# A gated mix of linear attention and a token MLP: the order and the queues of the first loads

## The chip, the cores and the metric

The kernel runs on one core of a Trainium2 chip. The metric is the device time of one execution in microseconds (us), as the median of several runs. A core has TensorE (PE in the profile: matmuls; PEld: its weight loads), VectorE (DVE), ScalarE (ACT), GpSimd (POOL) and SyncE (SP, which here only issues copies). Copies between the chip's memory and the core's buffers are carried out by 16 DMA engines; SP and ScalarE each have a queue of their own on which they issue them.

## The reference

For x of 2048 tokens by 512 features (bfloat16) the output is `g * a + (1 - g) * b`:

- `g = sigmoid(sum(x * gate_w))`, one number for each token.
- `a` is linear attention with 32 heads of 16 features: q, k, v from `x @ wqkv`, the feature map `phi(t) = where(t > 0, t + 1, exp(t)) + 1e-6` on q and k, `num = phi(q) @ (phi(k)^T v)`, divided by `phi(q) . sum(phi(k))`, then `@ wo`.
- `b` is an MLP over the tokens: `h = layernorm(x)` over the features, `u = gelu(h^T @ w1 + b1)` with w1 of 2048 by 1792, `y = u @ w2 + b2`, turned back.

So the first layer of the MLP sums over all 2048 tokens, and it needs the layernorm of every token before it ends.

## The kernel before

The 2048 tokens are 16 tiles of 128 (t = 0 to 15). A tile of x is 128 by 512 (128 KB); a tile of w1 in the first half of its columns, `w1A`, is 128 by 896 (224 KB).

The kernel begins with the MLP's first layer, first half. Seven accumulators `accA` (banks of TensorE's accumulation memory) each collect one 128-column block of w1A over the tokens. The loop over the first 12 tiles (lines 271 to 273) does seven matmuls for each tile, one to an accumulator; the last 4 tiles are done accumulator by accumulator, and each accumulator goes through a Gelu on ScalarE when it is complete. Then come the k projection with the sum `phi(k)^T x`, the second half of the first layer with the q projection between its blocks, and the second layer with the attention's output added in the same accumulators.

The matmuls of tile t need `xh[t]`, the normalised tile, and `w1A[t]`. The layernorm runs on VectorE, with one step on ScalarE: statistics (`bn_stats`, line 196), their aggregation (line 199), the standard deviation (Sqrt on ScalarE, line 201), its reciprocal (line 207) and the normalisation (line 209, written as "apply" here). VectorE's order is written out (lines 217 to 231): the statistics of tile t come before the apply of tile t - 1; for tiles 1 to 3 the statistics are in two halves, one before and one behind that apply. Instructions run in that order on each engine, so an apply waits for the next tile of x too.

Ahead of the matmuls stand 18 warm-up matmuls on a constant (line 183) and `vps` (line 186), a small matmul with an identity that turns 30 rows of bias (`b_rows`: 14 rows of b1, 16 rows of b2) into columns. Two copies on ScalarE (lines 229 and 230) move the result into `b1_sb` and `b2_sb` after the standard deviation of tile 1.

The copies in, all issued through `load` (line 124), are in program order on each queue. On ScalarE's queue: the rows of b1, the first 128 columns of w1A tile 0, the rows of b2; behind them on ScalarE come the load of the table for Sqrt and a first use of it. On the sync queue: x 0, x 1, the rest of w1A 0, and then x t + 1 and w1A t in turn; then the gate's row, the k weights, 16 transposing copies of x and the rest of the weights. The framework gives copies one of eight completion semaphores in turn, in the order of the program over both queues, and a copy waits on its queue until the copy eight before it has landed.

Of the kernel before, what the change touches and what calls it, by code (L numbers as in the profile page):

```python
# [16 lines left out]
def kernel(  # L17
# [13 lines left out]
    nc = tc.nc  # L31
    P = nc.NUM_PARTITIONS
# [9 lines left out]
    NT = S // P  # L42
    ND = D // P
    NF = F // P
# [4 lines left out]
    FA = NFA * P  # L49
    TAIL = 4  # L50

    x_view = X.rearrange("(t p) d -> p t d", p=P)
    o_view = O.rearrange("(t p) d -> p t d", p=P)
    wqkv_view = A_wqkv.rearrange("(k p) n -> p k n", p=P)
    w1_view = B_w1.rearrange("(t p) f -> p t f", p=P)
    w2_view = B_w2.rearrange("(f p) s -> p f s", p=P)
    b1_view = B_b1.rearrange("(f p) -> f p", p=P)
    b2_view = B_b2.rearrange("(t p) -> t p", p=P)
# [8 lines left out]
    def ptile(shape, dt, name):  # L67
        return persist.tile(shape, dt, name=name, tag=name)

    def bank(name):  # L70
        return psum.tile([P, SC], FP32, name=name, tag="bank")

    def mm(o, lhsT, rhs, start, stop, **kw):
        tc.keep_in_program_order(
            nc.tensor.matmul(o, lhsT=lhsT, rhs=rhs, start=start, stop=stop, **kw)  # L75
        )

    xr = ptile([P, NT, D], BF16, "xr")
# [17 lines left out]
    ident = ptile([P, P], BF16, "ident")  # L96
    gw_b = ptile([P, D], BF16, "gw_b")
    b_rows = ptile([NF + NT, P], BF16, "b_rows")
    b1_sb = ptile([P, NF], FP32, "b1_sb")
    b2_sb = ptile([P, NT], FP32, "b2_sb")  # L100
# [17 lines left out]
    w1A = wpool.tile([P, NT, FA], BF16, name="w1A", tag="w")  # L118
    w1B = wpool.tile([P, NT, FA], BF16, name="w1B", tag="w")

    pin = tc.keep_in_program_order

    def load(o, i, eng=None, **kw):
        pin((eng or nc.sync).dma_start(out=o, in_=i, **kw))

    def load_x(t0, t1):
        load(xr[:, t0:t1, :], x_view[:, t0:t1, :])

    def load_w1a(t):
        load(w1A[:, t, :], w1_view[:, t, 0:FA])  # L130


    tbl = work.tile([P, 1], FP32, name="tbl", tag="tbl", bufs=2)
    load(b_rows[0:NF, :], b1_view, nc.scalar)
    load(w1A[:, 0, 0:P], w1_view[:, 0, 0:P], nc.scalar)
    load(b_rows[NF : NF + NT, :], b2_view, nc.scalar)
    pin(nc.scalar.activation(out=tbl[:], in_=eps_t[:], func=ACT.Sqrt))

    load_x(0, 1)
    load_x(1, 2)  # L140
    load(w1A[:, 0, P:FA], w1_view[:, 0, P:FA])
    for t in range(1, NT):
        if t + 1 < NT:
            load_x(t + 1, t + 2)
        load_w1a(t)
    load(gw_b[:], gw_row_view.to_broadcast([P, D]))
    load(wk_sb[:], wqkv_view[:, :, D : 2 * D])
    for c in range(NSC):
# [11 lines left out]
    for j in range(ND):  # L160
# [10 lines left out]
        out=mask[:], in_=mask[:], compare_op=ALU.is_gt, fill=1.0,  # L171
# [3 lines left out]
        out=mask[:], in_=mask[:], compare_op=ALU.is_ge, fill=0.0,  # L175
# [4 lines left out]

    warm_ps = bank("warm_ps")
    one = nc.const_aps.tensor(1.0, [P, 256], BF16)
    for _ in range(18):
        mm(warm_ps[:, :256], one[:, 0:P], one, True, True)
    vps = bank("vps")
    mm(vps[:, : NF + NT], b_rows[:], ident[0 : NF + NT, 0 : NF + NT], True, True)

    BS = nc.vector.BN_STATS_DIM  # L190
# [2 lines left out]
    def ln_bn(t, d0, d1, h, parts):  # L193
        if h == 0:
            stats[t] = work.tile([P, parts, BS], FP32, name="stats", tag=f"stats{parts}", bufs=4)
        pin(nc.vector.bn_stats(out=stats[t][:, h, :], in_=xr[:, t, d0:d1]))  # L196

    def ln_aggr(t):
        pin(nc.vector.bn_aggr(out=mv[:, t, :], in_=stats[t][:]))
        pin(  # L200
            nc.scalar.activation(
                out=sd[:, t : t + 1], in_=mv[:, t, 1:2], func=ACT.Sqrt, bias=eps_t[:], scale=1.0
            )
        )

    def ln_apply(t):
        pin(nc.vector.reciprocal(out=rstd[:, t : t + 1], in_=sd[:, t : t + 1]))
        pin(
            nc.vector.tensor_scalar(
                out=xh[:, t, :], in0=xr[:, t, :],  # L210
                scalar1=mv[:, t, 0:1], scalar2=rstd[:, t : t + 1],
                op0=ALU.subtract, op1=ALU.mult,
            )
        )
# [4 lines left out]
    for t in range(1, NT):  # L219
        if t < HALVES:  # L220
            ln_bn(t, 0, D // 2, 0, 2)
            ln_apply(t - 1)
            ln_bn(t, D // 2, D, 1, 2)
        else:
            ln_bn(t, 0, D, 0, 1)
            ln_apply(t - 1)
        ln_aggr(t)
        if t == 1:
            pin(nc.scalar.copy(out=b1_sb[:], in_=vps[:, :NF]))
            pin(nc.scalar.copy(out=b2_sb[:], in_=vps[:, NF : NF + NT]))  # L230
    ln_apply(NT - 1)


    tbl = work.tile([P, 1], FP32, name="tbl", tag="tbl", bufs=2)
# [22 lines left out]
    def gelu(acc, j):  # L257
        pin(
            nc.scalar.activation(
                out=uT[:, j, :], in_=acc[:], func=ACT.Gelu_apprx_tanh,  # L260
                bias=b1_sb[:, j : j + 1], scale=1.0,
            )
        )
# [4 lines left out]
    def mlp1(acc, w, col, t, last):  # L268
        mm(acc[:], w[:, t, col : col + P], xh[:, t, :], t == 0, last)

    for t in range(NT - TAIL):
        for j in range(NFA):
            mlp1(accA[j], w1A, j * P, t, False)
    for j in range(NFA):
        for t in range(NT - TAIL, NT):
            mlp1(accA[j], w1A, j * P, t, t == NT - 1)
        gelu(accA[j], j)
# [53 lines left out]
    for i in range(ND):  # L331
# [4 lines left out]
            out=z_parts[:, 1, :], in0=zacc[:], in1=z_parts[:, 0, :], op=ALU.subtract  # L336
# [214 lines left out]
    t = NT - 1  # L551
# [35 lines left out]
```

## Time and profile before

| | us |
|---|---|
| median of 3 runs (163.14 to 163.45) | 163.24 |
| the profiled execution | 163.19 |
| its span, first to last instruction | 161.5 |
| TensorE busy with matmuls | 156.9 (97%) |
| VectorE busy | 117.6 (73%) |
| ScalarE busy | 53.1 (33%) |

The profile is of one execution. Busy time is counted by instruction; matmuls are pipelined and their ends are modelled, so their rate is read from the distance of their starts. The chain of work that ended last goes back from the last instruction, at each step to what released it. A line of the timeline has the start and the duration in us, the engine, the line of the kernel, the operation, what it writes and reads, the shape and the count, and in brackets the idle time before it and what ended it. An engine's name with a q (SPq, ACTq) is its issuing part: such a line is the issue of a copy, not its transfer.

### The profile page before, as it was taken

How to read it: one execution, taken by the hardware profiler on the slowest of the kernel's cores; microseconds unless marked ns; L12 is line 12 of the kernel's file. 1: busy time of each engine (PE TensorE's matmuls, PEld its weight loads, DVE VectorE, ACT ScalarE, POOL GpSimd, SP SyncE). 2: the span in 40 equal slices, each digit the busy share in tenths (PEclk: the TensorE clock that was granted, in tenths of full speed). 3: DMA queues.
4: the chain of work that ended last, by engine and by line, in shares of the span. 5: the costliest groups of instructions: out<-in, count | busy, mean ns of one | idle time of the engine just before them, and what ended most of it. 6: DMA issues, size and time to landing. Idle time of an engine off the chain costs nothing.

```text
span 161.5 us, 2192 instructions
## 1 busy us (share of the span) xinstructions
PE 156.9 (97%) x775; PEld 73.0 (45%) x789; DVE 117.6 (73%) x272; ACT 53.1 (33%) x91; POOL 1.5 (1%) x10
## 2 busy tenths in 40 slices
PE   7999999999999999999999999999999999999992
PEld 5444444444444445444444444444444444444452
DVE  2999989999999997998959999999999900000002
ACT  3222258962332124261348730000008330150140
POOL 3000000000000000000000000000000000000000
PEclk9999999999999999999999999999999999999999
DMA  4999996445699942169930103999445367360021
GB/s 139 279 351 341 335 186 139 108 105 102 165 394 380 265 136 81 37 211 381 334 67 0 39 32 80 345 392 296 153 69 162 91 196 233 71 189 4 0 97 33
DMA packets 36806, 28.33 MB, mean 175 GB/s; under 512 B 20412, under 2 KB 33084, under 8 KB 36796
## 3 DMA queue, kind: packets, MB, share of 16 engines
q1 hardware_dynamic: 36320, 27.90, 58.7%
q10 hardware_dynamic: 476, 0.30, 0.6%
q8 instruction: 6, 0.10, 0.3%
q14 instruction: 4, 0.03, 0.1%
HBM read 19.28 MB, written 4.46 MB: 147 GB/s over the span
## 4 chain that ended last, share of the span: by engine, by line
PE 97%; issue 1%; DVE 0%; DVEq 0%
PE yps L75 38%; PE accA L75 15%; PE accB L75 15%; PE qacc L75 9%; PE kacc L75 9%; PE Gps L75 8%; PE warm_ps L75 2%; PE kvps L75 0%; DVE ot L531 0%; PE w2ps L75 0%; PE vps L75 0%; DVEq L531 0%
## 5 line engine op out<-in xcount | busy, mean ns | idle before, releaser
L75 PE MATMUL yps<-uT,w2h 128*128 128x512 bf16 (+2 forms) x234 | 49.0, 366 | 0.2
L75 PEld LDWEIGHTS <-w2h 128*128 128x128 bf16 x238 | 22.8, 98 | 25.9
L524 ACT ACTIVATE ot<-yps,c,c 128x512 bf16<-128x512 f32 x15 | 11.5, 777 | 46.9 <-DVE pq L400 24.4
L75 PE MATMUL accB<-xh,w1B 128*128 128x512 bf16 x110 | 24.9, 379 | 0.1
L75 PE MATMUL accA<-xh,w1A 128*128 128x512 bf16 x110 | 24.4, 381 | 0.1
L531 DVE TENSOR_SCALAR ot<-yps,c,c 128x384 bf16<-128x384 f32 (+1 forms) x2 | 1.1, 544 | 29.0 <-PE yps L75 29.0
L75 PEld LDWEIGHTS <-xT 128*128 128x128 bf16 x128 | 12.4, 98 | 14.9 <-issue 0.2
L75 PEld LDWEIGHTS <-w1B 128*128 128x128 bf16 x112 | 10.9, 98 | 13.2
L75 PEld LDWEIGHTS <-w1A 128*128 128x128 bf16 x112 | 10.9, 98 | 13.2 <-issue 0.4
L75 PE MATMUL kacc<-wk_sb,xT 128*128 128x512 bf16 x63 | 15.7, 379 | 0.1
L75 PE MATMUL Gps<-pk,xr 128*128 128x512 bf16 x62 | 15.5, 379 | 0.1
L75 PE MATMUL yps<-W2sb,pqT 128*128 128x512 bf16 (+2 forms) x67 | 14.6, 366 | 0.1
L75 PE MATMUL qacc<-wq_sb,xT 128*128 128x512 bf16 x62 | 14.4, 379 | 0.1
L282 ACT ACTIVATE e<-qacc 128x512 bf16<-128x512 f32 x16 | 9.6, 597 | 12.2 <-PE qacc L75 8.0
L282 ACT ACTIVATE e<-kacc 128x512 bf16<-128x512 f32 x16 | 9.2, 598 | 12.7 <-PE kacc L75 7.0
L196 DVE BATCH_NORM_STATS2 stats<-xr 128x6 f32<-128x512 bf16 (+1 forms) x19 | 11.1, 582 | 2.1 <-DMA xr<-in_A_x_dram 2.1
L400 DVE SCALAR_TENSOR_TENSOR pq<-pq,odds,rd 128x512 bf16<-128x512 bf16 x16 | 12.0, 752 | 0.6
L396 DVE TENSOR_REDUCE den<-prod 128x32 f32<-128x544 f32 x16 | 11.5, 720 | 0.6
L289 DVE SCALAR_TENSOR_TENSOR pk<-kacc,e 128x512 bf16<-128x512 f32 x16 | 11.1, 692 | 1.0
L289 DVE SCALAR_TENSOR_TENSOR pq<-qacc,e 128x512 bf16<-128x512 f32 x16 | 11.1, 692 | 0.6
L241 DVE CUSTOM_DVE_ANT_0 junk<-xr,gw_b 128x512 bf16<-128x512 bf16 x16 | 11.0, 690 | 0.5
L284 DVE TENSOR_SCALAR e<-e 128x512 bf16<-128x512 bf16 x32 | 9.2, 288 | 2.8 <-ACT e L282 2.4
(54 smaller groups left out, 95.3 us busy)
## 6 DMA issues: line engine op xcount, KB each, us to landing
w2h<-in_B_w_dram SPq DMA_DIRECT2D x4, 1792.0 KB, 7.7
w1B<-in_B_w_dram SPq DMA_DIRECT2D x4, 896.0 KB, 8.3
w1A<-in_B_w_dram SPq DMA_DIRECT2D x15, 224.0 KB, 4.2
xr<-in_A_x_dram SPq DMA_DIRECT2D x16, 128.0 KB, 3.9
q_dram<-pq SPq DMA_DIRECT2D x16, 128.0 KB, 1.8
out_dram<-ot SPq DMA_DIRECT2D x15, 128.0 KB, 1.8
wk_sb<-in_A_wqkv_dram SPq DMA_DIRECT2D x1, 512.0 KB, 7.0
wv_sb<-in_A_wqkv_dram SPq DMA_DIRECT2D x1, 512.0 KB, 13.5
```

Of the source, the lines that this page charges most:

```text
L75: nc.tensor.matmul(o, lhsT=lhsT, rhs=rhs, start=start, stop=stop, **kw)
L196: pin(nc.vector.bn_stats(out=stats[t][:, h, :], in_=xr[:, t, d0:d1]))
L241: nc.vector.tensor_tensor_reduce(out=junk[:], in0=xr[:, t, :], in1=gw_b[:], scale=1.0, scalar=0.0, op0=ALU.mult, op1=ALU.add, accum_out=gp ...
L282: pin(nc.scalar.activation(out=e[:], in_=acc[:], func=ACT.Exp))
L284: nc.vector.tensor_scalar(out=e[:], in0=e[:], scalar1=1.0, scalar2=PHI_EPS, op0=ALU.min, op1=ALU.add)
L289: nc.vector.scalar_tensor_tensor(out=o, in0=acc[:], scalar=0.0, in1=e[:], op0=ALU.max, op1=ALU.add)
L396: pin(nc.vector.tensor_reduce(out=den[:], in_=prod[:], op=ALU.add, axis=AX.X))
L400: nc.vector.scalar_tensor_tensor(out=heads, in0=heads, scalar=odds[:, t : t + 1], in1=rd[:].unsqueeze(2).to_broadcast([P, NH, HEAD]), op0= ...
L524: nc.scalar.activation(out=ot[:, d0:d1], in_=yps[:, d0:d1], func=ACT.Identity, scale=c1[:, t : t + 1], bias=c2[:, t : t + 1],)
L531: nc.vector.tensor_scalar(out=ot[:, d0:d1], in0=yps[:, d0:d1], scalar1=c1[:, t : t + 1], scalar2=c2[:, t : t + 1], op0=ALU.mult, op1=ALU.add,)
```

## The change

x tile 0 is loaded as two halves of 64 tokens, the first on the sync queue, the second on ScalarE's; x tile 1 comes whole on ScalarE's queue, behind that half. The sync queue then carries w1A 0 (now one copy) and w1A 1, and from t = 2 on x t and w1A t in turn. The two copies of bias rows go on the sync queue behind w1A 3. One warm-up matmul is dropped. The matmul `vps` moves behind the seven matmuls of tile 8, and the two copies to `b1_sb` and `b2_sb` come, on ScalarE, behind the load of the Gelu table and before the first Gelu.

```diff
-    load(b_rows[0:NF, :], b1_view, nc.scalar)
-    load(w1A[:, 0, 0:P], w1_view[:, 0, 0:P], nc.scalar)
-    load(b_rows[NF : NF + NT, :], b2_view, nc.scalar)
+    HP = P // 2
+    load(xr[0:HP, 0, :], x_view[0:HP, 0, :])
+    load(xr[HP:P, 0, :], x_view[HP:P, 0, :], nc.scalar)
+    load(xr[:, 1, :], x_view[:, 1, :], nc.scalar)
     pin(nc.scalar.activation(out=tbl[:], in_=eps_t[:], func=ACT.Sqrt))
-
-    load_x(0, 1)
-    load_x(1, 2)
-    load(w1A[:, 0, P:FA], w1_view[:, 0, P:FA])
-    for t in range(1, NT):
-        if t + 1 < NT:
-            load_x(t + 1, t + 2)
+    load_w1a(0)
+    load_w1a(1)
+    for t in range(2, NT):
+        load_x(t, t + 1)
         load_w1a(t)
+        if t == 3:
+            load(b_rows[0:NF, :], b1_view)
+            load(b_rows[NF : NF + NT, :], b2_view)
...
-    for _ in range(18):
+    for _ in range(17):
         mm(warm_ps[:, :256], one[:, 0:P], one, True, True)
-    vps = bank("vps")
-    mm(vps[:, : NF + NT], b_rows[:], ident[0 : NF + NT, 0 : NF + NT], True, True)
...
         ln_aggr(t)
-        if t == 1:
-            pin(nc.scalar.copy(out=b1_sb[:], in_=vps[:, :NF]))
-            pin(nc.scalar.copy(out=b2_sb[:], in_=vps[:, NF : NF + NT]))
     ln_apply(NT - 1)
...
     for t in range(NT - TAIL):
         for j in range(NFA):
             mlp1(accA[j], w1A, j * P, t, False)
+        if t == NT // 2:
+
+            vps = bank("vps")
+            mm(vps[:, : NF + NT], b_rows[:], ident[0 : NF + NT, 0 : NF + NT], True, True)
+            pin(nc.scalar.copy(out=b1_sb[:], in_=vps[:, :NF]))
+            pin(nc.scalar.copy(out=b2_sb[:], in_=vps[:, NF : NF + NT]))
```

## The prediction

> **What bounds the kernel now.** I read the page's busy line first, then the chain that ended last, then the timeline of the first 24 us, then the landing times of the single copies there.
>
> ```profile
> PE 156.9 (97%) x775; PEld 73.0 (45%) x789; DVE 117.6 (73%) x272; ACT 53.1 (33%) x91; POOL 1.5 (1%) x10
> ...
> 0.83 4.00 PE warm_ps L75 x18
> 4.86 0.18 PE vps L75
> 5.03 6.77 PE accA L75 x30
> ```
>
> TensorE (PE) is busy 97% of the span and the chain runs through it from 0.83 us on. Nothing in the change takes a matmul of the computation away, so it can act only on the moment at which the first layer (accA) runs without a gap. What sets that moment stands in the timeline (start, duration, engine):
>
> ```profile
> 0.79 0.67 ACTq L124 DMA_DIRECT2D b_rows<-in_B_b_dram  x1
> 1.49 0.37 ACTq L124 DMA_DIRECT2D w1A<-in_B_w_dram  x1
> 2.19 0.43 SPq L124 DMA_DIRECT2D xr<-in_A_x_dram  x1
> 3.01 0.69 DVE L196 BATCH_NORM_STATS2 stats<-xr 128x6 f32<-128x512 bf16 x1 [2.08 <-DMA xr<-in_A_x_dram]
> 3.84 0.40 DVE L196 BATCH_NORM_STATS2 stats<-xr 128x6 f32<-128x256 bf16 x1
> 4.28 0.16 DVE L207 RECIPROCAL rstd<-sd 128x1 f32<-128x1 f32 x1
> 4.34 0.33 SPq L124 DMA_DIRECT2D xr<-in_A_x_dram  x1
> 4.48 0.41 DVE L209 TENSOR_SCALAR xh<-xr,mv,rstd 128x512 bf16<-128x512 bf16 x1
> 4.96 11.37 PE L75 MATMUL accA<-xh,w1A 128*128 128x512 bf16 x50
> 5.39 0.37 DVE L196 BATCH_NORM_STATS2 stats<-xr 128x6 f32<-128x256 bf16 x1
> 6.97 0.43 DVE L196 BATCH_NORM_STATS2 stats<-xr 128x6 f32<-128x256 bf16 x1
> 8.50 0.64 DVE L196 BATCH_NORM_STATS2 stats<-xr 128x6 f32<-128x512 bf16 x1
> 9.24 0.41 DVE L209 TENSOR_SCALAR xh<-xr,mv,rstd 128x512 bf16<-128x512 bf16 x1
> 9.70 6.35 PEld L75 LDWEIGHTS <-w1A 128*128 128x128 bf16 x30 [0.15 <-issue]
> ```
>
> VectorE (DVE) idles 2.08 us for x tile 0, then works without a pause to the end of xh tile 3 at 9.24 + 0.41 = 9.65. The first statistics on x tiles 1, 2, 3 and 4 stand at 3.84, 5.39, 6.97 and 8.50; each x tile has landed by then. PE starts tile 0 at 4.96, just after xh 0 (4.89), and tile 3 at 9.70, just after xh 3 (9.65), where its weight load shows the only pause. A tile costs PE seven matmuls of 0.216 us (24.38 us for 112), 1.51 us, and DVE, once whole-tile statistics begin, 1.18 us (12.77 minus 11.59, two starts of the apply). So from tile 4 on DVE gains on PE. **The path is x tile 0 to tile 3 through DVE; whatever delays DVE there delays the end one for one.** It returns once: xh 15 is ready at 23.27 + 0.41 = 23.68 and PE wants it at 9.70 + 66 x 0.216 = 23.95, a cover of 0.27 us.
>
> The landings, as KB and us from issue to landing:
>
> ```profile
> w1A<-in_B_w_dram ACTq DMA_DIRECT2D x1, 32.0 KB, 2.8
> ...
> b_rows<-in_B_b_dram ACTq DMA_DIRECT2D x1, 4.0 KB, 2.8
> ```
>
> Single copies on the sync queue (SP), from the trace's answers on xr and w1A over narrow stretches: x 0 2.2, x 1 2.2 (lands 3.5), x 2 2.9 (5.1), w1 1 3.9 (6.6), w1 2 4.0 (7.6), x 4 3.7 (8.0), w1 3 3.9 (8.6). The DMA engines are already 0.80, 0.93, 0.78, 0.90, 0.97 busy in the five microseconds from 2 to 7.
>
> **The change, part by part.**
>
> *x tile 0 in halves.* The halves' statistics wait for both. Each half's issue can take SP's 0.40 to 0.43; ScalarE's first copy took 0.67. If that 0.67 belongs to the queue's first copy, the second half is no earlier than now (landing 2.99); if not, half the rows behind each issue save at most about half of the 0.40 us that one issue takes, 0.2 us. Gain 0 to 0.2; I take 0.1, between. It is worth something only if x 1 is there too, because the DVE order puts statistics of x 1 ahead of the apply of tile 0.
>
> *x tile 1 on ScalarE's queue.* It is issued second there: at 1.49 (after 0.67) or about 1.25 (after 0.43), instead of 1.26 on SP. Landing after 2.2 us (SP's first copies) gives 3.5 to 3.7; after 2.8 us (both measured copies of this queue) 4.1 to 4.3. The nearest rows are this queue's, and those were smaller copies: I take 4.1. DVE then starts at 4.12 instead of 3.84: +0.28 for xh 0 (5.17).
>
> *w1 tiles 0 and 1 ahead of x 2.* x 2 is still the fourth copy on SP, at 2.19, but now has x 0, x 1, all of w1 0 and w1 1 before it: 224 KB more. In the trace of before that same set of copies ends with w1 1 at 6.6, when part of x 3 had been moved too; its bytes (some 850 kB) were moved by about 5.4 (262 + 275 + 203 kB in the stretches from 2 to 5, then 271 per us), and x 2 itself landed about 0.7 us behind its bytes, which gives 6.1. Two queues issue the set 0.47 us (one SP slot) sooner, which, used fully, gives 5.6. At best nothing is lost (5.1). I take 5.8, between 5.6 and 6.1, against a need of 5.39: **+0.4 us on DVE**, which takes in the 0.28 of x 1. Likewise x 3 now takes the place of w1 2 (7.6, less 0.47: 7.1) against 6.97, and x 4 that of w1 3 plus the bias rows: +0.2 and about +0.4, the same shift, not added to it.
>
> *Bias rows behind tile 3.* Two issues on SP, 0.43 each (ScalarE's rows: 0.67 and 0.44), ahead of x 4, w1 4 and all later copies. x 4 is the tenth copy instead of the eighth: 0.79 + 9 x 0.47 = 5.02, up to 5.26, instead of 4.34; with 3.7 us it lands at 8.7 to 9.0. Needed at 8.50 + 0.4 = 8.9, so covered by the shift already counted, or a 0.1 more. x 5 goes from 5.18 to about 6.0, landing 9.7, needed at 9.66 + 0.4: covered. Each ninth copy waits for the landing of the one eight before it (the SP waits on w1A landings are 2.0 us in all, seven times), so later ones follow the landings, not the count. The gate row, wk and the transposes move by at most a slot, 0.5 us; the eighth transpose is issued near 28.4, lands 2.8 later and is wanted at 32.8, 1.6 us of cover.
>
> *vps moves from before tile 0 to behind tile 8.* Before, it ran 4.86 to 4.96 while PE waited for xh 0 anyway: removing it gains nothing unless xh 0 comes before 4.9. Behind tile 8 PE has no gap, so its place is paid: 0.11 us (from its start to the next matmul) at most, and at least 0.02 (a 64-column matmul of kvps, 32 in 0.62 us). The 128-column weight load after it needs about 0.1 (98 ns) and a 30-column matmul can't hide it: **+0.1 us**. The bias rows have landed long before (18.5 us against about 9).
>
> *The two bias copies on ScalarE* (0.15 and 0.17) now stand after the Gelu table load and ahead of the seven Gelus. The first Gelu starts 0.3 later; a Gelu takes 0.72, its accumulator comes each 0.86, so the lag is gone after three. No PE instruction waits for it. Cost 0.
>
> *17 warm-up matmuls for 18, and the Sqrt table sooner.* A warm-up has 256 columns and takes 0.21 us, half the rate of accA's 512 in 0.216. The first accA takes 546 ns, the median 379: it was still mostly slow, so the fast rate comes at about 5.3. A warm-up less changes nothing while xh 0 is later than 4.6. The table load (2.36 to 3.64) moves up by about one issue, 0.4; the first use is at 3.95, no gain.
>
> One rule speaks against the split. The row first: the DMA engines are 0.80 to 0.93 busy from 2 to 4 us with one queue carrying nearly all bytes, so little is left for a second one. The Trainium skill, "DMA: Bandwidth & Descriptors", section "Issuing engines are not separate DMA queues", says the same more strictly: copies of any issuing engine share the same 16 DMA engines and a second issuer saves issue time alone. By it, the x 0 gain would be at most the one issue slot and x 2 would keep the whole wait for w1 1 (6.1, +0.7). This trace has no two large copies on two queues to show it.
>
> The sum: xh 3 and tile 3 +0.4, vps +0.1 = +0.5 us. PE's own early start does not help: the matmuls before tile 3 then wait for xh 1 to 3. The profiled execution took 163.19 us (span 161.5 and 1.7 around it), 0.05 under the median of 163.24: 163.7.
>
> **The rivals.**
>
> *Not slower: x 1 and x 2 come in time.* If ScalarE's queue delivers like SP's (x 1 by 3.7) and x 2 by 5.3, DVE keeps its pace or gains the 0.1 to 0.2 of x 0. PE then starts up to 0.2 earlier, but at half rate until 5.3, so at tile 3 it has 0.1 plus the pause of 0.04: -0.14 to 0, and vps +0.1: 163.1 to 163.4. For it: the DMA share of 0.78 from 4 to 5 leaves room. Against: both copies of this queue took 2.8. It decides at x 1 landing before 3.85 and x 2 before 5.4; each 0.1 beyond costs 0.1.
>
> *The x tiles wait fully behind w1.* x 2 lands like w1 1 did (6.6), or x 4 at 9.7 behind bias rows that issue slowly: +0.8 to +1.2 on DVE, vps 0.1: 164.1 to 164.5. For it: the early w1 copies took 3.9, x 2 2.9.
>
> *TensorE stays slow longer.* PE is idle from 4.4 to 5.2 or more, where it idled 0.2. If the fast rate needs unbroken work and comes 4.5 us after the first real matmul (as it came 4.5 us after 0.83), 4.4 us at half rate cost 2.2: 165.9. Against: accA's first matmul sped up in spite of the gap at vps.
>
> **How the numbers follow.** Main case, 163.4 to 164.0: 0.45. Not slower: 0.27. Full wait: 0.16. Slow clock: 0.04. A gain that I don't see: 0.08. A difference of 0.2% (0.33 us) is about what a measurement of this kernel tells from none. Below 162.9: the unseen gain and 0.02 of the second case, 0.10. Within: 0.25 of the second case and 0.07 of the main one, 0.32. Above 163.57: 0.38 + 0.16 + 0.04 = 0.58. The range 163.1 to 164.4 leaves out the unseen gain, the slow clock and the ends.
>
> **What would show it.** Right: statistics of x 1 start near 4.1 with a DMA wait, those of x 2 near 5.8, xh 3 ends near 10.05, tile 3 starts about 0.4 later, vps costs 0.1 between two accA matmuls, nothing later differs. Wrong: DVE without waits for xr, or accA starting before 4.9.

## The result and the profile after

The changed kernel takes 165.66 us (median of six runs, 164.22 to 166.05) against 163.34 for the kernel before in the same comparison: ratio 1.0115, 95% interval 1.0085 to 1.0145. By the medians it is 2.3 us slower; the ratio, estimated over all the executions and so not the quotient of the medians, gives 1.9 (1.4 to 2.4). The forecast was 0.4 to 0.5 slower, with a range of 163.1 to 164.4. The profiled execution took 166.05 us, 2.86 more than the profiled one of before.

The page of the changed kernel, busy times and two groups (line, engine, operation, tiles, shape, count, then busy us, mean ns, idle us before and what ended it), and behind them the accA group of the kernel before:

```profile
PE 159.1 (97%) x788; PEld 73.3 (45%) x788; DVE 117.7 (72%) x272; ACT 53.2 (32%) x91; POOL 1.6 (1%) x10
...
L75 PE MATMUL accA<-xh,w1A 128*128 128x512 bf16 x112 | 26.2, 397 | 1.5 <-DVE xh L208 1.5
...
L195 DVE BATCH_NORM_STATS2 stats<-xr 128x6 f32<-128x512 bf16 (+1 forms) x19 | 11.0, 581 | 3.3 <-DMA xr<-in_A_x_dram 3.3
```

```profile
L75 PE MATMUL accA<-xh,w1A 128*128 128x512 bf16 x110 | 24.4, 381 | 0.1
```

TensorE is as full as before, 97%, and that hides the loss. The accA matmuls occupy 26.2 us instead of 24.4 (there are 112 in both kernels; two records are missing in the profile of before), TensorE idles 1.5 us for xh, and VectorE waits 3.3 us for x instead of 2.1. The chain that ended last (start, duration, what) no longer begins on TensorE:

```profile
0.80 0.56 ACTq L124
...
1.40 3.69 DMA xr<-in_A_x_dram
...
5.65 0.42 DVE xh L208
...
6.11 15.46 PE accA L75 x63
```

It begins with ScalarE's queue: the half of x 0 is issued there first, and behind it x 1, issued at 1.40, takes 3.7 us to land. The timeline shows the same place from VectorE's and TensorE's side:

```profile
3.23 0.69 DVE L195 BATCH_NORM_STATS2 stats<-xr 128x6 f32<-128x512 bf16 x1 [2.29 <-DMA xr<-in_A_x_dram]
...
5.12 0.43 DVE L195 BATCH_NORM_STATS2 stats<-xr 128x6 f32<-128x256 bf16 x1 [0.98 <-DMA xr<-in_A_x_dram]
...
6.11 10.06 PE L75 MATMUL accA<-xh,w1A 128*128 128x512 bf16 x38 [1.49 <-DVE xh L208]
```

Statistics of x 0 start at 3.23 instead of 3.01, those of x 1 at 5.12 instead of 3.84. The apply of tile 0 stands behind them in VectorE's order, so accA starts at 6.11 instead of 4.96: +1.15 us. Then the matmuls are slow. One microsecond of each kernel (its length, then busy and count of PE, PEld, DVE, ACT, POOL, then the granted clock, DMA share and GB/s), first of the changed kernel:

```profile
7.00:8.00 1.00, 1.00 (x4) 0.36 (x3) 0.93 (x4) 0.00 (x0) 0.00 (x0) 1.00 1.01 252
```

and of the kernel before:

```profile
7.00:8.00 1.00, 1.00 (x7) 0.45 (x5) 0.96 (x5) 0.29 (x1) 0.00 (x0) 1.00 1.04 344
```

Both show PE busy 1.00 and a granted clock of 1.00, but four matmuls are touched in it instead of seven. The trace has the start of each matmul: the first ones lie 0.427 us apart, and from 9.75 on 0.216. From 6.11 to 9.75 nine matmuls start (distances 0.381, seven of 0.427, 0.273): 3.64 us where nine at the fast rate take 1.94, so 1.7 are lost. The kernel before lost 0.2 in the same stretch (0.17 on its first matmul, 0.04 of waiting at tile 3): +1.5. The last piece is vps behind tile 8, whose price is worked out at its experiment: +0.2. The sum 1.15 + 1.5 + 0.2 = 2.85 stands against 2.86 measured.

Between executions the changed kernel varies from 164.2 to 166.05, the kernel before from 163.1 to 163.9. The experiments show that the slow matmuls make most of that spread: with them prevented it goes. Only one execution of each kernel has a profile; that others of them had slow matmuls is read from their times.

### The profile page after: what moved, and what is told of

Its sections match the earlier page's. It is cut to its first block, busy times and chain, and to the rows that moved or that the text cites. A ratio compares the mean times of both kernels' runs of the same rounds, so it can differ in the third digit from the quotient of the medians.

```text
span 164.3 us, 2205 instructions
## 1 busy us (share of the span) xinstructions
PE 159.1 (97%) x788; PEld 73.3 (45%) x788; DVE 117.7 (72%) x272; ACT 53.2 (32%) x91; POOL 1.6 (1%) x10
## 4 chain that ended last, share of the span: by engine, by line
PE 94%; DMA 2%; DVE 1%; ACTq 0%; issue 0%; DVEq 0%
PE yps L75 38%; PE accA L75 16%; PE accB L75 15%; PE qacc L75 9%; PE Gps L75 8%; PE kacc L75 8%; DMA xr<-in_A_x_dram 2%; PE kvps L75 0%; ACTq L124 0%; DVE stats L195 0%; DVE xh L208 0%; DVE ot L534 0%; PE w2ps L75 0%; PE vps L75 0%; DVE rstd L206 0%
## 5 line engine op out<-in xcount | busy, mean ns | idle before, releaser
L75 PE MATMUL accA<-xh,w1A 128*128 128x512 bf16 x112 | 26.2, 397 | 1.5 <-DVE xh L208 1.5
```

## The experiments

Theory A: x 1 is late because of where it is issued; TensorE, idle after its warm-up, then runs its first matmuls at half rate for up to four microseconds. Theory B, its rival: w1 0 and w1 1 ahead of the x tiles on the sync queue cost it. A third question was what each part is worth alone. Every kernel was timed beside the kernel before, whose median was 163.34 to 163.44 in these comparisons.

### Idle time before the first matmul, with no load moved

```diff
 (kernel before)
-    for _ in range(18):
+    for _ in range(12):
```

> The kernel before with 12 warm-up matmuls instead of 18 and nothing else: TensorE idles from 3.4 to 4.9, about as long as in the changed kernel, but no load or VectorE instruction moves. Theory A: accA still starts at 4.96 and its first seven to nine matmuls run at half rate in some or all executions, +1.0 to +1.7 us: 164.2 to 164.9. Rival (idle time of that length does not matter to the rate): 163.2 to 163.4.

Measured: 165.11 us (163.60 to 165.35), ratio 1.0082 (1.0052 to 1.0112). TensorE's timeline:

```profile
0.84 2.72 PE L75 MATMUL warm_ps<-const-bfloat16-1.0 128*128 128x256 bf16 x12 [0.84 <-PEq L571]
4.79 0.18 PE L75 MATMUL vps<-ident,b_rows 30*128 30x30 bf16 x1 [1.24 <-DMA b_rows<-in_B_b_dram]
4.92 8.35 PE L75 MATMUL accA<-xh,w1A 128*128 128x512 bf16 x28
```

and the same stretch of the kernel before:

```profile
4.96 8.35 PE L75 MATMUL accA<-xh,w1A 128*128 128x512 bf16 x36
```

accA starts when it did before (4.92), but 28 matmuls fill 8.35 us, where 36 did in the kernel before; the full rate comes at 9.43. Nothing but TensorE's work ahead of the first matmul was changed: theory A's second half holds. The single executions (163.6, 164.3, four of 165.1 to 165.4) show that how much is lost varies from one execution to the next.

### The changed kernel with the idle time filled

```diff
 (changed kernel)
-    for _ in range(17):
+    for _ in range(25):
```

> The changed kernel with 25 warm-up matmuls instead of 17, so that TensorE works until xh 0 comes near 6.1. Theory A: the loads and VectorE do the same as in the changed kernel (accA starts near 6.1), but TensorE is fast from the first accA matmul; of the 2.9 us that the profiled execution lost, the 1.5 us of slow matmuls go and the 1.15 of the late start and 0.1 of vps stay: 164.3 to 164.6, with little spread between executions. Rival: the slow matmuls have nothing to do with the idle time (they follow the loads, or the switch comes at a time of its own): 165.5 to 166, as the changed kernel.

Measured: 164.30 us (163.96 to 164.57), ratio 1.0054 (1.0039 to 1.0070).

```profile
0.84 4.90 PE L75 MATMUL warm_ps<-const-bfloat16-1.0 128*128 128x256 bf16 x25 [0.84 <-PEq L574]
5.69 7.50 PE L75 MATMUL accA<-xh,w1A 128*128 128x512 bf16 x32
```

Eight warm-up matmuls more make the kernel 1.36 us faster (165.66 to 164.30) and take the spread away. x 1 happened to land sooner in this profile (statistics at 4.70), and accA started at 5.69. The last five warm-ups start 0.11 us apart instead of 0.213, so the full rate came between 4.84 and 5.02, in work that 17 warm-ups would not have reached; no accA matmul was slow. So of the 2.3 us about 1.4 are slow matmuls, about 0.9 the late loads and vps.

The same on a variant whose executions were all slow: w1 in turn with x, everything else as changed.

```diff
 (changed kernel)
-    load_w1a(1)
-    for t in range(2, NT):
-        load_x(t, t + 1)
+    for t in range(1, NT):
+        if t + 1 < NT:
+            load_x(t + 1, t + 2)
         load_w1a(t)
```

> The changed kernel with the order on the sync queue undone: first half of x 0, w1 0, x 2, w1 1, x 3, w1 2, x 4, w1 3, bias rows. Halves, x 1 on ScalarE's queue, vps and 17 warm-ups as changed. Theory A: x 1 is as late as in the changed kernel (4.6 to 5.1), because w1 0 is still ahead of it; x 2 comes a slot sooner (5.2 to 5.5). accA starts at 5.7 to 6.1 and the slow matmuls stay: 165 to 166. Theory B (w1 1 ahead of x 2 is what costs): 163.5 to 164.

Measured: 165.86 us (165.46 to 166.02), ratio 1.0155 (1.0137 to 1.0173). Then the same with 25 warm-ups:

```diff
 (the variant with w1 in turn)
-    for _ in range(17):
+    for _ in range(25):
```

> The variant with w1 in turn (halves, x 1 on ScalarE's queue, 165.9 with eight slow matmuls after a start at 5.4) with 25 warm-up matmuls instead of 17; no load moves. Theory A: only TensorE's idle time goes, so the slow matmuls go: 163.9 to 164.5, with little spread. Rival (the 165.9 of that variant comes from its loads): 165.5 or more.

Measured: 164.24 us (163.88 to 164.50), ratio 1.0045 (1.0032 to 1.0059). TensorE's first lines, with 17 and with 25:

```profile
5.42 7.79 PE L75 MATMUL accA<-xh,w1A 128*128 128x512 bf16 x27 [0.80 <-DVE xh L208]
```

```profile
5.43 7.91 PE L75 MATMUL accA<-xh,w1A 128*128 128x512 bf16 x35
```

Two executions whose accA starts within 0.01 us of each other: 27 matmuls in 7.8 us against 35 in 7.9, and medians 1.6 us apart. Theory B expected 163.5 to 164 from putting w1 back in turn; it gave 165.86. In this profile x 1 was there sooner (its statistics at 4.31, accA at 5.42 instead of 6.11), but nothing of that reaches the time while the matmuls are slow.

Whether the one dropped warm-up is to blame by itself:

```diff
 (kernel before)
-    for _ in range(18):
+    for _ in range(17):
```

> The kernel before with 17 warm-up matmuls instead of 18 and nothing else: TensorE idles from 4.4 instead of 4.6 to 4.9. The prediction's step: no effect, 163.2 to 163.5. Rival: one warm-up less is already enough to put off the fast rate in some executions: some above 164.2.

Measured: 163.34 us (163.09 to 163.64), ratio 0.9994 (0.9985 to 1.0004). No effect on the time, as predicted; 17 are too few only because the loads come later.

### Which part makes x 1 late

```diff
 (changed kernel)
-    load(xr[:, 1, :], x_view[:, 1, :], nc.scalar)
+    load(xr[:, 1, :], x_view[:, 1, :])
```

> The changed kernel with one part undone: x 1 goes on the sync queue behind the first half of x 0; all else as changed. Theory A (x 1 is late because it is on ScalarE's queue, and TensorE, idle for 1.5 us, then runs slowly until 9.6): x 1 lands near 3.7 instead of 5.1, the normalised tile 0 is ready near 5.1 instead of 6.06, TensorE idles 0.6 us instead of 1.5. x 2 then still comes behind w1 0 and w1 1 (6.1 to 6.5 against a need of 5.4 before), so tile 3 starts about 0.8 to 1.0 late; with 0.1 for vps 164.1 to 164.4, if the fast rate comes soon after 5.3. Theory B (w1 0 and w1 1 ahead of the x tiles delay everything, the queue of x 1 does not matter): x 1 lands no earlier than 4.7 and the time stays above 165.

Measured: 164.69 us (164.39 to 166.14), ratio 1.0100 (1.0065 to 1.0136). In the profiled execution x 1 lands 2.4 us after its issue at 1.43, its statistics start at 4.11 without a wait, and those of x 2 at 6.22 after one of 0.47. Theory A's landings held, and theory B's (x 1 no earlier than 4.7) did not; the time is 0.3 above theory A's range; two of the six executions (166.1) still had the slow matmuls, or so their time suggests.

The opposite: x 1 on ScalarE's queue and nothing else.

```diff
 (kernel before)
     load(b_rows[0:NF, :], b1_view, nc.scalar)
+    load(xr[:, 1, :], x_view[:, 1, :], nc.scalar)
     load(w1A[:, 0, 0:P], w1_view[:, 0, 0:P], nc.scalar)
...
     load_x(0, 1)
-    load_x(1, 2)
```

> The kernel before with x 1 moved to ScalarE's queue, second there behind the rows of b1; x 0 whole on the sync queue, w1 in turn with x, vps early, 18 warm-ups. Theory A (the second copy on ScalarE's queue comes late by itself, whether x 0 is halved or not): x 1 lands at 4.2 to 5.0 instead of 3.5, accA starts 0.3 to 1.0 late and some executions have slow matmuls: 163.9 to 165.5. Rival (it was the halves, issued at the same time on both queues, that held x 1 up): x 1 lands by 3.8, and the time is 163.2 to 163.6.

Measured: 165.67 us (163.91 to 166.19; four executions near 164.0, six from 165.6 up), ratio 1.0106 (1.0069 to 1.0143). This one move costs as much as the whole change. VectorE's line for x 1:

```profile
4.43 0.43 DVE L196 BATCH_NORM_STATS2 stats<-xr 128x6 f32<-128x256 bf16 x1 [0.54 <-DMA xr<-in_A_x_dram]
```

x 0, whole, is as early as before (statistics at 2.98), and x 1, issued at 1.50 on ScalarE's queue, comes at 4.4: 2.9 us after its issue, where the sync queue's second copy took 2.2. Moving it there is enough; the halves aren't needed for it. Whether the queue delays it, or w1 0, which is now issued at 1.27, ahead of it, is not separated here. The edit has a side effect: the rows of b2 are now the fourth copy on ScalarE's queue, and vps, which stands ahead of accA in TensorE's order, waited for them:

```profile
5.95 0.17 PE L75 MATMUL vps<-ident,b_rows 30*128 30x30 bf16 x1 [1.32 <-DMA b_rows<-in_B_b_dram]
```

xh 0 was ready at 5.37, so some 0.6 us of TensorE's idle time are the bias rows', and the 2.3 us are not all x 1's. (The profiled execution, 164.11, is one of the four.)

What runs beside x 1 was tried by issuing x 2 in place of w1 0:

```diff
 (changed kernel)
+    load_x(2, 3)
     load_w1a(0)
     load_w1a(1)
     for t in range(2, NT):
-        load_x(t, t + 1)
+        if t + 1 < NT:
+            load_x(t + 1, t + 2)
         load_w1a(t)
```

> The changed kernel with x 2 issued on the sync queue ahead of w1 0 (first half of x 0, x 2, w1 0, w1 1, x 3, w1 2, x 4, ...); x 1 second on ScalarE's queue as changed. Theory A, refined (x 1 waits for the slow first rows of w1 0): beside x 2, whose rows are served in some 50 ns each, x 1 lands at 3.9 to 4.2 instead of 5.1, accA starts at 5.1 to 5.3 or when w1 0 lands (4.9 to 5.2): 163.8 to 164.3 where the fast rate comes soon, above 165 where not. Rival (the second copy on ScalarE's queue is late whatever runs beside it): x 1 lands at 4.7 or later, 165 to 166.

Measured: 164.24 us (164.07 to 166.17; four executions up to 164.24, three from 165.39 up, the profiled one among them), ratio 1.0091 (1.0054 to 1.0129). Statistics of x 1 start at 4.59, between the two expectations. In the other profiles with x 1 second behind the half they start at 5.12 and 4.70 with the loads as changed, and at 4.31 and 4.29, without a wait, with w1 in turn, where w1 0 is beside x 1 as well. So it is not shown that x 1 waits for the first rows of w1 0, and what moves its landing between 4.3 and 5.1 stays open.

x 0 whole, x 1 first on ScalarE's queue:

```diff
 (changed kernel)
-    HP = P // 2
-    load(xr[0:HP, 0, :], x_view[0:HP, 0, :])
-    load(xr[HP:P, 0, :], x_view[HP:P, 0, :], nc.scalar)
+    load_x(0, 1)
     load(xr[:, 1, :], x_view[:, 1, :], nc.scalar)
```

> The changed kernel with the halves undone: x 0 whole on the sync queue, so x 1 is the first copy on ScalarE's queue instead of the second; w1 0 and w1 1 still ahead of x 2, 17 warm-ups. Theory A, refined (x 1 was late because, issued second and 0.77 long, its transfer waited until the first rows of w1 0 were through): x 1, issued at 0.8, is served before w1 0 and lands near 3.3 to 3.7; x 0 lands near 3.0 as before; accA starts near 4.95 to 5.1. What stays is x 2 behind w1 1 (near 6, tile 3 0.6 to 0.8 late) and vps 0.1: 163.9 to 164.4, some executions above 165 where the fast rate comes late. Theory B (ScalarE's queue is slow for any large copy): x 1 lands after 4.3 and the time is 165 or more.

Measured: 164.29 us (164.12 to 164.33), ratio 1.0058 (1.0042 to 1.0073). x 1 no longer waits, but now x 0 is late:

```profile
3.53 0.69 DVE L193 BATCH_NORM_STATS2 stats<-xr 128x6 f32<-128x512 bf16 x1 [2.60 <-DMA xr<-in_A_x_dram]
4.36 0.39 DVE L193 BATCH_NORM_STATS2 stats<-xr 128x6 f32<-128x256 bf16 x1
```

Of two tiles issued at the same moment on two queues, x 0 comes 0.5 us later than alone (3.01), and x 1 is there by 4.36. Expected was 3.0 for x 0; that was wrong. (In the last experiment below, where both landings are recorded, they are 2.7 and 2.9 us from the issue.)

No execution of the five (164.1 to 164.3) has the time that slow matmuls would give it, while all five of the variant with w1 in turn (165.5 to 166.0) have, although TensorE idled longer here. The warm-ups show the difference. First the variant with w1 in turn, where TensorE then idled 0.80 us, and behind it this kernel:

```profile
0.84 3.79 PE L75 MATMUL warm_ps<-const-bfloat16-1.0 128*128 128x256 bf16 x17 [0.84 <-PEq L574]
```

```profile
0.84 3.33 PE L75 MATMUL warm_ps<-const-bfloat16-1.0 128*128 128x256 bf16 x17 [0.84 <-PEq L572]
5.46 1.67 PE L75 MATMUL accA<-xh,w1A 128*128 128x512 bf16 x7 [1.29 <-DVE xh L206]
```

The same 17 matmuls took 3.33 us instead of 3.79: their last four start 0.11 us apart instead of 0.213. The full rate had come at 3.56, ahead of the idle time, and idling for 1.29 us did not undo it.

The other profiles, one execution each, agree. In five of the sixteen the rate rises among the warm-ups (this one, both with 25 warm-ups, the one with 20 at the end, and x 1 alone moved, where TensorE idled 1.32 us), and none of these has a slow accA matmul. In the other eleven it had not risen by then: the seven in which TensorE idled 0.67 us or less have the full rate by 6.5, the four in which it idled 0.80 or more (w1 in turn 0.80, x 2 ahead of w1 0.95, 12 warm-ups 1.24, changed kernel 1.49) only at 8.9 to 9.75. So an idle time does harm where the full rate has not come yet. When it comes varies between profiles with the same warm-ups; why all five executions of this kernel seem to have had it in time is not shown.

### The price of the other parts

vps alone:

```diff
 (kernel before)
-    vps = bank("vps")
-    mm(vps[:, : NF + NT], b_rows[:], ident[0 : NF + NT, 0 : NF + NT], True, True)
...
             mlp1(accA[j], w1A, j * P, t, False)
+        if t == NT // 2:
+            vps = bank("vps")
...
```

> The kernel before with vps and the two bias copies moved behind tile 8 and nothing else; all copies in are issued as before, 18 warm-ups. The prediction's step: TensorE pays vps where it now stands, 0.1 more than before: 163.4 to 163.6. If the earlier 0.4 of the whole bias part was vps, 163.7 or more; if this is 163.4 to 163.6, the rest of that 0.4 came from the moved copies of bias rows.

Measured: 163.80 us (163.34 to 164.04), ratio 1.0017 (1.0006 to 1.0028), so +0.3, with an interval of 0.1 to 0.5. The step on TensorE is seen without that spread in the timeline of the changed kernel around vps:

```profile
17.74 3.83 PE L75 MATMUL accA<-xh,w1A 128*128 128x512 bf16 x17
21.50 0.18 PE L75 MATMUL vps<-ident,b_rows 30*128 30x30 bf16 x1
21.62 2.55 PE L75 MATMUL accA<-xh,w1A 128*128 128x512 bf16 x11
```

Of the 17 matmuls the last starts at 17.74 + 16 x 0.216 = 21.19 and the next accA at 21.62: 0.43 instead of 0.216. vps costs 0.21 us, one whole matmul, and not 0.1: besides the 0.12 from its start to the next matmul, it starts 0.1 later than an accA matmul would have. In the profiled execution of this kernel the first accA matmuls were slow for longer than in the kernel before (distances 0.378, 0.427, 0.426, 0.310): without vps, TensorE idles from 4.6 to 5.0. These four lose 0.7 us against the full rate, 0.5 more than in the kernel before; with the 0.2 of vps that is the 0.73 by which this execution (163.92) is longer than the profiled one of before.

The whole bias part:

```diff
 (kernel before, with vps as above)
-    load(b_rows[0:NF, :], b1_view, nc.scalar)
-    load(b_rows[NF : NF + NT, :], b2_view, nc.scalar)
...
         load_w1a(t)
+        if t == 3:
+            load(b_rows[0:NF, :], b1_view)
+            load(b_rows[NF : NF + NT, :], b2_view)
```

> The kernel before with the bias part of the change alone: both copies of bias rows on the sync queue behind w1 3, vps behind tile 8, the two copies before the first Gelu; x and w1 as before, 18 warm-ups. The prediction's step: vps costs 0.1 where it now stands, x 5 and later copies come one to two slots later and are covered: 163.3 to 163.4. Rival: the two slots on the sync queue, or the Gelus behind the two copies, cost more than 0.3: 163.6 or more.

Measured: 163.80 us (163.43 to 164.63), ratio 1.0024 (1.0011 to 1.0037). The same median as vps alone, so the times show no cost of the moved copies. The profiles lose in different places, though: here x 2 came late (its statistics at 5.92, after a wait of 0.32 us, where they stood at 5.43 with vps alone), and xh 3 with it; in the profile of vps alone it was slow matmuls that cost 0.5. So the rival, that the moved copies cost something, is neither shown nor excluded.

The order on the sync queue alone:

```diff
 (kernel before)
-    for t in range(1, NT):
-        if t + 1 < NT:
-            load_x(t + 1, t + 2)
+    load_w1a(1)
+    for t in range(2, NT):
+        load_x(t, t + 1)
         load_w1a(t)
```

> The kernel before with only the order on the sync queue changed: w1 1 ahead of x 2, then x and w1 in turn (x 0, x 1, w1 0, w1 1, x 2, w1 2, ...); x 2 is a slot later than in the changed kernel. This is the prediction's largest step by itself: there x 2 was to land at 5.8 and cost 0.4; a slot later here, 6.0 to 6.5, 0.6 to 1.1 on VectorE and the time 163.9 to 164.5. accA starts at 4.96 as before, so no slow matmuls. Rival (x tiles behind a w1 tile cost nothing): 163.2 to 163.5.

Measured: 163.86 us (163.59 to 164.09), ratio 1.0030 (1.0018 to 1.0043), +0.5.

```profile
5.96 0.43 DVE L196 BATCH_NORM_STATS2 stats<-xr 128x6 f32<-128x256 bf16 x1 [0.57 <-DMA xr<-in_A_x_dram]
```

Statistics of x 2 start at 5.96 instead of 5.39, after a wait of 0.57. xh 3 ends at 10.10 instead of 9.65, and the profiled execution (163.63) is 0.44 longer than that of before: what VectorE is late at tile 3, the kernel loses.

The halves alone, on top of vps behind tile 8:

```diff
 (kernel with vps behind tile 8)
+    HP = P // 2
+    load(xr[HP:P, 0, :], x_view[HP:P, 0, :], nc.scalar)
     load(b_rows[0:NF, :], b1_view, nc.scalar)
...
-    load_x(0, 1)
+    load(xr[0:HP, 0, :], x_view[0:HP, 0, :])
```

> As the kernel with vps behind tile 8, plus x 0 in two halves, the first on the sync queue, the second first on ScalarE's queue; x 1 and all else as before. The prediction's step: x 0 lands up to 0.2 sooner, at most 0.1 gained: 163.3 to 163.5. Theory A, from the profiles so far (the halves took 0.57 each to issue where a whole tile takes 0.40, and statistics of x 0 never started before 3.23): x 0 lands 0.2 to 0.3 later and so does everything behind it, 0.2 to 0.4 above the kernel with vps behind tile 8.

Measured: 164.22 us (163.92 to 164.45), ratio to the kernel before 1.0047 (1.0034 to 1.0060), 0.4 above the kernel without halves. Statistics of x 0, first without, then with halves:

```profile
3.05 0.69 DVE L194 BATCH_NORM_STATS2 stats<-xr 128x6 f32<-128x512 bf16 x1 [2.11 <-DMA xr<-in_A_x_dram]
```

```profile
3.32 0.69 DVE L196 BATCH_NORM_STATS2 stats<-xr 128x6 f32<-128x512 bf16 x1 [2.39 <-DMA xr<-in_A_x_dram]
```

The halves come 0.27 later than the whole. That is not all of what this edit does: ScalarE now issues four copies ahead of its table load, which starts at 3.12 instead of 2.37, and VectorE waits for the first standard deviation:

```profile
4.84 0.16 DVE L207 RECIPROCAL rstd<-sd 128x1 f32<-128x1 f32 x1 [0.30 <-ACT sd L201]
```

accA starts at 5.50 instead of 4.99, 0.51 late, of which the landing of the halves explains about half. In the changed kernel, with two copies ahead of the table load, that wait does not appear. In the six other profiles with halves the statistics of x 0 start at 3.23 to 3.49.

### A version of the parts that looked harmless

```diff
 (kernel before)
-    load(b_rows[0:NF, :], b1_view, nc.scalar)
-    load(w1A[:, 0, 0:P], w1_view[:, 0, 0:P], nc.scalar)
-    load(b_rows[NF : NF + NT, :], b2_view, nc.scalar)
+    load_x(0, 1)
+    load(xr[:, 1, :], x_view[:, 1, :], nc.scalar)
+    load(b_rows[0:NF, :], b1_view, nc.scalar)
+    load(b_rows[NF : NF + NT, :], b2_view, nc.scalar)
...
-    load_x(0, 1)
-    load_x(1, 2)
-    load(w1A[:, 0, P:FA], w1_view[:, 0, P:FA])
+    load_w1a(0)
...
-    for _ in range(18):
+    for _ in range(20):
 (vps behind tile 8)
```

> A version made of the parts that theory A calls harmless: x 0 whole and first on the sync queue, x 1 whole and first on ScalarE's queue, the two bias copies behind it there; sync queue in turn (w1 0, x 2, w1 1, x 3, ...), each one slot sooner than before; 20 warm-ups, so that TensorE works until xh 0 comes; vps behind tile 8. Theory A: x 0 lands near 3.0, x 1 near 3.5, x 2 near 5, accA starts near 5.0, and vps costs 0.1: 163.2 to 163.6, like the kernel before. If the loads on two queues hold each other up in spite of that (w1 0 landing after 5): 164 or more.

Measured: 163.88 us (163.71 to 164.17), ratio 1.0034 (1.0021 to 1.0046). Its statistics of x 0 start at 3.49, again 0.5 late beside x 1, and accA starts at 5.43, at full rate (the last warm-ups were already fast). It beats the changed kernel by 1.8 us and loses to the kernel before by 0.5. No variant tried was faster than the kernel before by more than the noise.

## Why the prediction was wrong

- **The direction was right, the path in part.** The loss arises between x 0 and tile 3 of the matmuls, VectorE's written order passes a late x 1 on to tile 0, and behind that place only vps costs anything. But "whatever delays DVE there delays the end one for one" held only while TensorE waits for VectorE. In the profiled execution of the changed kernel TensorE itself is last: xh 3 is ready at 10.81, and TensorE reaches tile 3 at 12.3.
- **x 1 on ScalarE's queue: mis-sized.** "I take 4.1", bounded by 3.5 and 4.3; statistics started at 5.12, 1.28 us late instead of 0.28. The bounds came from the 2.8 us of that queue's small copies. A whole tile second there took 2.9 us in one profile and 3.7 in another; why, stays open.
- **x 0 in halves: wrong in sign.** A gain of 0 to 0.2 was allowed, no loss. x 0 came 0.27 us later; the run with the halves was 0.4 us longer, part of it by the later table load. No reason had been given that excluded a loss. The issue of a half takes 0.55 to 0.58 us, that of a whole tile 0.40, and nothing showed that a half issues no slower.
- **w1 0 and w1 1 ahead of x 2: right in mechanism and nearly in size.** +0.4 forecast from a landing at 5.8; alone 0.57 on VectorE and +0.5 of time. In the profiled execution of the changed kernel it is hidden: x 1 was so late that VectorE did not wait for x 2 as well, and TensorE, slow until 9.75, reaches tile 3 only at 9.75 + 12 x 0.216 = 12.3.
- **vps behind tile 8: mis-sized.** 0.1 forecast, 0.21 measured on TensorE. The working took the time from vps to the next matmul and left out that vps itself starts later than a matmul of its kind before it would let it.
- **Bias rows and copies on ScalarE: not contradicted**; the times show no cost, one profile has a later x 2. **17 warm-ups ("A warm-up less changes nothing while xh 0 is later than 4.6"): right** only while the loads are as before. The sum had no term for the rate of the first matmuls, and that is its largest miss.
- **TensorE stays slow longer: the rival that decided.** It was given 0.04 and a price of 2.2 us. It happened, and cost 1.4 us in the median (25 warm-ups against 17) and 1.5 in the profiled execution. That its 165.9 lies near the measured 165.66 is partly luck: it added 2.2 to the 0.5 of the main case, while the profiled execution has 1.5 of slow matmuls beside 1.15 of a late start and 0.2 of vps. "Against: accA's first matmul sped up in spite of the gap at vps" compared a gap of 0.2 us with the 0.8 or more that the working itself expected (1.5 were measured). That was no ground for a chance so small.
- **The rule weighed in the prediction.** The Trainium skill, "DMA: Bandwidth & Descriptors", section "Issuing engines are not separate DMA queues", says that copies from all issuers run interleaved on the same 16 DMA engines and that a second issuer saves only issue time. The runs agree that a second queue moves no data sooner: x 0 and x 1 issued together, x 0 came 0.5 us later than alone and x 1 no sooner than the 3.5 of before. In this kernel, where x 0 is needed first, that sharing was a loss.
- **On TensorE's rate.** The Trainium skill, "TensorE: Matmul & The Clock Gate", section "Part 1: The HAM clock gate", says that the full rate comes after about 3.4 us of work seen in a window that runs freely. The profiles show the full rate between 3.56 and 9.75 us, with the first warm-up at 0.84 in all of them, so from 2.7 us of work on, which is sooner than those 3.4. It came at about 5.3 us in the kernel before and 9.6 in the changed one, 4.3 apart, and the kernel with 12 warm-ups varies by 1.75 us between executions with no load moved; that fits a window whose place is a matter of chance. No run shows the window itself.

## What to carry to other kernels

Count what a late first operand does to the matmul rate, not only the wait: an idle time of about one microsecond ahead of the full rate cost up to 1.7 us here, more than the wait itself, and extra warm-up matmuls that reach to the first real one bought it back. Whether the rate had risen before the gap can be read from the distance of the warm-ups' own starts. Spreading the first loads over two queues can delay the one that is needed first: here x 0 was earliest when it was whole and no other large copy was issued at the same moment. A written order that puts the next tile's work ahead of this tile's last step makes the second load as urgent as the first.

## What was not expected of the hardware

- The granted clock read 1.00 in stretches in which matmuls of 512 columns started 0.427 us apart instead of 0.216. Only the distance of starts, or their count in a stretch, showed the slow rate.
- Two half-tile copies issued at the same time on two queues took 0.55 to 0.58 us each to issue; two whole tiles 0.39 to 0.41.
- A lone matmul of 30 columns between matmuls of 512 cost 0.21 us, as much as one of them.
